# Seven half products for the second matmul of group 4 in a convolution and MLP kernel

## The chip, the core and the metric

The kernel runs on one core of a Trainium2 chip. The metric is the device time of one execution in microseconds (us). Before the change it is 1014.25 us, the median of three runs from 1014.22 to 1014.34. The profile is of a single execution whose span is 1012.3 us.

The names of the engines in the profile: PE is TensorE's matmul and PEld its weight load, DVE is VectorE, ACT is ScalarE, POOL is GpSimd, SP is SyncE, which here only issues transfers.

## What is computed

The input `x` has 8 sequences of 4224 tokens with 192 channels. A causal convolution of seven taps (one set of softmax weights for each of eight heads of 24 channels) gives `x`, and a block with layer norm and two matmuls is added to it:

```python
w = exp(weight - max); w = w / (sum(w) + 1e-09)          # (8 heads, 7 taps)
x = einsum('hk,bskhg->bshg', w, x_unf)                   # the convolution
xn = (x - mu) / np.sqrt(var + 1e-06) * g_ln
ch = np.maximum(xn @ w_ch1, 0.0) @ w_ch2                 # 192 -> 768 -> 192
return x + ch
```

All of it is in float32.

## The kernel before

**Tiling.** Each sequence is spread over 128 partitions, 33 consecutive tokens to a partition. The work goes in 18 groups (`groups`, lines 65 to 73): the first sequence has four small ones (6, 8, 9 and 10 tokens a partition, groups 0 to 3), and every later sequence has one of 16 and one of 17 tokens. Group 4 is the first of the 16-token ones; group 5 follows with 17, group 6 with 16, and so on to group 17.

**Stages of a group.** `load_x` (line 102) brings in the tokens. `first_tap` (line 324, done on ACT at line 336) and `conv` (line 338, DVE, line 346) make the convolution `y`: eight heads by six further taps are 48 DVE instructions. `transpose` (line 351, DVE, line 357) turns `y` in blocks of 32 by 32 into `yt`. `stats` (line 374) computes the scale of each token on DVE. `up` (line 427) is the first matmul: line 457 on TensorE into PSUM tiles `ph`, and line 469 on ACT, the Relu into the hidden tile `ht`. The mean is already taken out of the weights, and the scale is applied to the result afterwards, on ACT at line 624. Then comes the second matmul, which exists in two forms:

- `down` (line 479): the plain one. For each of six blocks of 32 output channels, 24 matmuls at line 493 (six hidden chunks of 128 by four partition blocks of 32) add up into a PSUM tile `po`. `finish` (line 649) has DVE transpose each `po` into the output tile `ot` (line 653).
- `down_fast` (line 537): hidden channels, output channels and tokens are each cut into two halves, and the product of these two-by-two block matrices is made from seven products of half blocks instead of eight, in the manner of Strassen and Winograd. That takes sums of the input halves (DVE, `sums_early` at lines 522 and 523, `sums_late` at 533 and 535), sums of the weight halves (`w2_sums`, line 502, done once), the seven calls of `product` (line 550, matmuls at 555 into PSUM tiles `pd`, and an eviction by ACT at 560 for each of three banks), and sums of the results (DVE, 585 and 598) before the transposes into `ot` (line 600).

**What selects the form.** The table `fast` (lines 76 and 77) gives the number of tokens of each group that go the fast way. Before the change it is 0 for groups 0 to 4 and all tokens for groups 5 to 16; the last group takes 12 of its 17 that way. The table also decides how `up` lays out `ht` and where the Relu writes.

**Order of the work.** The order on each engine is written out by hand: each engine runs its instructions in the order in which the program emits them, and the loop at line 675 is that order. In a group with a fast second matmul the convolution of the next group is cut up, with the sums between its parts; in a group with the plain one it is emitted in one piece. These lines carry it (shortened):

```python
if fast[g]:
    conv(g + 1, 1, 4)
    sums_early(g, (0,))
    conv(g + 1, 4, 5)
    sums_early(g, (1, 2))
    parts = down_fast(g)      # in it: first_tap(g + 2), conv(g + 1, 5, 6), sums_late, line 585
    conv(g + 1, 6, 7)
else:
    conv(g + 1)
transpose(g + 1); store_y(g + 1); stats(g + 1)
# fast: finish_fast(g); plain: down(g), finish(g), first_tap(g + 2)
```

**Buffers.** `yt`, `ht`, `ot`, the sums `s1`, `cs` and `part` have one buffer each, `xg` and `y` two. The eight PSUM banks are shared: `up` takes four at a time, `down` one for each block of channels, `down_fast` six.

Of the kernel before, what the change touches and what calls it, by code (L numbers as in the profile page):

```python
# [16 lines left out]
def kernel(  # L17
# [47 lines left out]
    groups = []  # L65
# [7 lines left out]
    NG = len(groups)  # L73


    fast = {g: groups[g][2] if g >= 5 else 0 for g in range(NG)}
    fast[NG - 1] = J - 5
    NFAST = max(fast.values())
    T = C // 2
# [678 lines left out]
```

## Time and profile before

| | before |
|---|---|
| time, median of 3 runs | 1014.25 us |
| span of the profiled execution | 1012.3 us |
| PE busy | 1000.9 us (99%) |
| DVE busy | 900.4 us (89%) |
| ACT busy | 490.5 us (48%) |
| first matmul (`ph`, L457), share of the chain that ended last | 51.0% |
| half products (`pd`, L555), share of the chain | 35.4% |
| plain second matmul (`po`, L493), share of the chain | 10.3% |

A row of the page's groups names the line, the engine, the operation, the tiles it writes and reads, their shape, and then the busy time of all such instructions, the mean of one in ns, and the idle time of the engine just ahead of them. A float32 matmul leaves two records, so 288 records of L493 are 144 matmuls. The chain that ended last is followed back from the last instruction, at each step to what released it; in order of time it shows in what pieces the span is spent. Where an instruction has a time and an arrow in brackets, its engine stood idle that long before it, and what is named behind the arrow ended the wait.

### The profile page before, as it was taken

To read this page: it belongs to the slowest core of one execution; us is meant where nothing else is said; L and a number is where in the kernel's file an instruction comes from. 1 tells how busy PE (TensorE), PEld (TensorE's weight loads), DVE (VectorE), ACT (ScalarE), POOL (GpSimd) and SP (SyncE) were. 2 spreads that over 40 slices of the span, in tenths; PEclk is the share of its full clock that TensorE was granted. 3 is DMA by queue.
4 is the path that set the end of the run, shared out by engine and by line. 5 is a ranking of instruction groups with operands and counts; after the bars stand their busy time and mean duration, and the time that the engine had idled before them with its cause. 6 is when DMAs were issued, how large, how long until landed. Compare 5 with 4: busy or idle time off the path is not lost.

```text
span 1012.3 us, 34807 instructions
## 1 busy us (share of the span) xinstructions
PE 1000.9 (99%) x15628; PEld 648.8 (64%) x15628; DVE 900.4 (89%) x1766; ACT 490.5 (48%) x1306; POOL 41.1 (4%) x59
## 2 busy tenths in 40 slices
PE   7999999999999999999999999999999999999997
PEld 6887654358545775458754686556854578545786
DVE  7998798955999999999999999989999999999645
ACT  6455344416445454555536455364644546454451
POOL 1001000000000000000000000000000000000000
PEclk9999999999999999999999999999999999999999
DMA  5242550502323433123332331334122343112031
GB/s 196 98 170 63 158 148 38 171 26 44 92 89 59 158 65 150 33 45 150 64 150 50 114 95 33 150 67 159 34 79 104 68 158 64 64 33 37 3 65 69
DMA packets 12068, 91.42 MB, mean 90 GB/s; under 512 B 1679, under 2 KB 2447, under 8 KB 7950
## 3 DMA queue, kind: packets, MB, share of 16 engines
q1 hardware_dynamic: 6718, 64.91, 16.7%
q0 software_dynamic: 4896, 24.28, 14.0%
q8 instruction: 122, 2.00, 0.8%
q14 instruction: 28, 0.23, 0.1%
q10 hardware_dynamic: 304, 0.00, 0.0%
HBM read 38.95 MB, written 50.23 MB: 88 GB/s over the span
## 4 chain that ended last, share of the span: by engine, by line
PE 97%; DVE 2%; DMA 0%; ACT 0%; issue 0%; DVEq 0%; ACTq 0%
PE ph L457 51%; PE pd L555 35%; PE po L493 10%; DVE y L346 1%; DMA taps<-in_weight_dram 0%; DVE y L636 0%; ACT room L266 0%; DVE room L197 0%; DVE yt L357 0%; DVE room L194 0%; ACT room L181 0%; DVE ot L653 0%; ACT room L189 0%; DVE room L186 0%; DVE room L180 0%
## 5 line engine op out<-in xcount | busy, mean ns | idle before, releaser
L457 PE MATMUL ph<-yt,w 32*128 32x256 f32 (+6 forms) x7200 | 517.1, 443 | 1.0 <-DVE yt L357 1.0
L457 PEld LDWEIGHTS ph<-yt,w 32*128 32x128 f32 x7200 | 364.3, 185 | 151.2 <-issue 118.6
L346 DVE SCALAR_TENSOR_TENSOR y<-xg,taps,y 128x384 f32<-128x384 f32 (+5 forms) x852 | 429.0, 580 | 0.0
L469 ACT ACTIVATE ht<-ph 128x256 f32<-128x256 f32 (+6 forms) x600 | 222.7, 457 | 268.9 <-PE ph L457 265.5
L555 PE MATMUL pd<-ht,w 128*32 128x256 f32 (+2 forms) x2808 | 158.0, 382 | 0.0
L555 PE MATMUL pd<-ht,w2sums 128*32 128x256 f32 (+2 forms) x2808 | 155.3, 381 | 0.0
L555 PEld LDWEIGHTS pd<-ht,w 128*32 128x32 f32 x2808 | 89.8, 110 | 66.6 <-issue 7.0
L555 PEld LDWEIGHTS pd<-ht,w2sums 128*32 128x32 f32 x2808 | 91.1, 110 | 61.8
L560 ACT COPY cs<-pd 128x272 f32<-128x272 f32 (+2 forms) x156 | 58.7, 376 | 111.3 <-PE pd L555 111.3
L493 PE MATMUL po<-ht,w 128*32 128x192 f32 (+5 forms) x1728 | 106.0, 406 | 0.0
L522 DVE TENSOR_TENSOR s<-ht 128x1088 f32<-128x1088 f32 (+2 forms) x39 | 48.1, 1233 | 53.5 <-ACT ht L469 53.5
L624 ACT ACTIVATE ot<-ot,r 128x192 f32<-128x192 f32 x247 | 93.1, 471 | 0.0
L493 PEld LDWEIGHTS po<-ht,w 128*32 128x32 f32 x1728 | 55.6, 110 | 49.5 <-issue 22.1
L560 ACT COPY part<-pd 128x272 f32<-128x272 f32 (+2 forms) x117 | 43.9, 375 | 88.0 <-PE pd L555 88.0
L336 ACT ACTIVATE y<-xg,taps 128x384 f32<-128x384 f32 (+5 forms) x142 | 74.1, 591 | 20.7 <-DVE st L371 16.3
L371 DVE BATCH_NORM_STATS2 st<-y 128x6 f32<-128x192 f32 x264 | 69.7, 341 | 0.0
L357 DVE STREAM_TRANSPOSE yt<-y 128x3072 f32<-128x3072 f32 (+5 forms) x18 | 56.0, 3112 | 1.4 <-DVE y L346 0.5
L628 POOL DMA_DIRECT2D out_dram<-ot x34 | 29.5, 883 | 665.6 <-ACT ht L469 348.7
L555 PE MATMUL pd<-s,w2sums 128*32 128x272 f32 (+2 forms) x936 | 53.4, 381 | 0.0
L600 DVE STREAM_TRANSPOSE ot<-cs 128x544 f32<-128x544 f32 (+2 forms) x78 | 50.0, 690 | 2.7 <-ACT cs L560 1.0
L523 DVE TENSOR_TENSOR ht<-ht 128x1088 f32<-128x1088 f32 (+2 forms) x39 | 48.2, 1235 | 2.2
L533 DVE TENSOR_TENSOR ht<-s,ht 128x1088 f32<-128x1088 f32 (+2 forms) x39 | 45.7, 1226 | 0.9 <-PE pd L555 0.9
(75 smaller groups left out, 271.6 us busy)
## 6 DMA issues: line engine op xcount, KB each, us to landing
xg<-in_x_dram SPq DMA_DIRECT2D x7, 2208.0 KB, 12.4
out_dram<-ot POOLq DMA_DIRECT2D x20, 768.0 KB, 6.5
xg<-in_x_dram SPq DMA_DIRECT2D x7, 2112.0 KB, 12.0
out_dram<-y SPq DMA_DIRECT2D x7, 1536.0 KB, 6.0
out_dram<-y SPq DMA_DIRECT2D x6, 1632.0 KB, 6.2
out_dram<-ot POOLq DMA_DIRECT2D x6, 864.0 KB, 6.9
xg<-in_x_dram SPq DMA_DIRECT2D x1, 1536.0 KB, 8.5
xg<-in_x_dram SPq DMA_DIRECT2D x1, 1440.0 KB, 6.9
```

Source lines behind the costliest of these rows:

```text
L336: nc.scalar.mul(dst, src, tap)
L346: nc.vector.scalar_tensor_tensor(out=y[g][:, 0:n, cs], in0=t[:, k : k + n, cs], scalar=taps[:, h, k : k + 1], in1=y[g][:, 0:n, cs], op0=AL ...
L357: nc.vector.transpose(yt[g][:, 0:n].rearrange("p j c t -> p (j c t)"), y[g][:, 0:n].rearrange("p j d -> p (j d)"),)
L371: nc.vector.bn_stats(out=sums[g][:, j, :], in_=y[g][:, j, :])
L457: nc.tensor.matmul(ph[q][:, 0:w], w1[rows, c, fs], t[rows, js, c, :], start=(c == 0), stop=(c == NC - 1),)
L469: nc.scalar.activation(dst, src, AF.Relu)
L493: nc.tensor.matmul(bank[C * q : C * q + C, 0:w], w2[:, f, C * c : C * c + C], t[:, f, q, js.start - fast[g] : js.stop - fast[g], :], start ...
L523: nc.vector.tensor_tensor(a[:, 1, 0, f], a[:, 0, 0, f], a[:, 1, 0, f], op=ALU.subtract)
L555: nc.tensor.matmul(dst[C * q : C * q + C, 0:w], right[:, f, C * c : C * c + C], left[:, f, q], start=(first and f == 0), stop=(f == FC - 1 ...
L560: nc.scalar.copy(to[:, c], dst[:, 0:w].rearrange("p (j t) -> p j t", t=T))
L600: nc.vector.transpose(ot[:, 0:n, C * c : C * c + C], cs[:, c].rearrange("p j h t -> p j (h t)"))
L624: nc.scalar.mul(ots[g][:, j, :], ots[g][:, j, :], rstd[g][:, j : j + 1])
```

## The change

Group 4 gets the fast second matmul too. Its 16 tokens take the seven half products, its Relus write the halved layout, and the convolution of group 5 is cut up around the sums, in the order that groups 6, 8 and so on have. It is meant to spare TensorE an eighth of the multiplications of this group's second matmul. The shape of the buffers does not change.

```diff
-    fast = {g: groups[g][2] if g >= 5 else 0 for g in range(NG)}
+    fast = {g: groups[g][2] if g >= 4 else 0 for g in range(NG)}
     fast[NG - 1] = J - 5
     NFAST = max(fast.values())
```

In the order of the instructions, that replaces on TensorE six runs of 24 matmuls of 512 columns by 252 matmuls of 256 columns. On DVE the 48 instructions of the convolution of group 5 are cut into runs of 24, 8, 8 and 8, with the sums between them, and six transposes at line 653 give way to the sums at 585 and 598 and six transposes at line 600. On ACT 21 evictions are added, and the first tap of group 6 is cut into four pairs between them.

## The prediction

> **What bounds the kernel now.** I read the page first, its busy times and its slices, then the chain of work that ended last, then VectorE (DVE) and ScalarE (ACT) in order of time around group 4. From the page:
>
> ```profile
> PE 1000.9 (99%) x15628; PEld 648.8 (64%) x15628; DVE 900.4 (89%) x1766; ACT 490.5 (48%) x1306; POOL 41.1 (4%) x59
> PE   7999999999999999999999999999999999999997
> DVE  7998798955999999999999999989999999999645
> ```
>
> TensorE is busy in every slice and DVE almost as much, except in slices 4 to 10, above all 9 and 10 (202 to 253 us: the second matmul of group 4 and the start of group 5). So TensorE sets the time, and DVE could take over wherever it gets more work. The chain, in order of time (start, length, what), shows group 4 to the start of group 7:
>
> ```profile
> 157.06 31.11 PE ph L457 x288
> 188.17 31.04 PE po L493 x288
> 219.21 33.21 PE ph L457 x576
> 252.42 29.01 PE pd L555 x504
> 281.43 31.11 PE ph L457 x288
> 312.55 27.33 PE pd L555 x504
> 339.88 33.21 PE ph L457 x576
> ```
>
> Each piece starts where the last one ends. Group 4 has its first matmul (L457) and then the plain second matmul (L493, tile po); group 6, with the same 16 tokens, has the seven half products (L555, tile pd) in its place. From 27.16 to 1005.63 us the chain holds TensorE work alone, so a microsecond less in one of these pieces is a microsecond less in the end, unless TensorE then waits. DVE in order of time, with the waits in brackets:
>
> ```profile
> 166.47 26.69 DVE L346 SCALAR_TENSOR_TENSOR y<-xg,taps,y 128x408 f32<-128x408 f32 x48
> 208.97 0.72 DVE L653 STREAM_TRANSPOSE ot<-po 128x512 f32<-128x512 f32 x1 [2.69 <-PE po L493]
> 214.12 0.72 DVE L653 STREAM_TRANSPOSE ot<-po 128x512 f32<-128x512 f32 x1 [4.43 <-PE po L493]
> 219.28 0.72 DVE L653 STREAM_TRANSPOSE ot<-po 128x512 f32<-128x512 f32 x1 [4.43 <-PE po L493]
> 242.79 1.29 DVE L522 TENSOR_TENSOR s<-ht 128x1088 f32<-128x1088 f32 x1 [10.12 <-ACT ht L469]
> 253.79 1.29 DVE L522 TENSOR_TENSOR s<-ht 128x1088 f32<-128x1088 f32 x1 [1.62 <-ACT ht L469]
> ...
> 304.36 1.23 DVE L522 TENSOR_TENSOR s<-ht 128x1024 f32<-128x1024 f32 x1 [1.44 <-ACT ht L469]
> 314.66 1.23 DVE L522 TENSOR_TENSOR s<-ht 128x1024 f32<-128x1024 f32 x1 [0.92 <-ACT ht L469]
> 333.73 3.58 DVE L357 STREAM_TRANSPOSE yt<-y 128x3264 f32<-128x3264 f32 x1
> ```
>
> In groups 4 and 5 DVE stands idle for 2.69 + 4.43 + 4.43 + 10.12 + 1.62 = 23.29 us. In group 6 it waits only 1.44 and 0.92, both for the Relus that its sums read: that is the settled rhythm, the same at group 16 (1.44 and 0.91).
>
> **What the Trainium skill says.** "Perfetto Trace Analysis", Identifying the Most-Contended Engine, warns that matmul busy share says little of the distance to roofline, while for Vector and Scalar the occupancy serves. Here the first half matters: 99% does not mean that no work can be taken away, and the chain, not the share, shows that the piece counts. "TensorE: Matmul & The Clock Gate", table at its head: ACT and DVE run strictly first in, first out, TensorE alone may pull weight loads ahead. The trace agrees: DVE sits in front of L522 with taps queued behind it, and in the 27.33 us of group 6's products 16.17 us of weight loads lie beside the matmuls. "VectorE: DVE Perf Modes", Side-by-side: one element a cycle in the plain mode plus about 150 cycles of setting up and 8 of fill at 0.96 GHz; for 1024 elements an estimate of 1182 / 0.96 = 1231 ns. The row of L522 with 1024 elements has 1223 ns: agreed, and I use the row.
>
> **The change part by part.**
> TensorE. Out go 144 matmuls of 512 columns (288 records: two for each). In come 7 products x 3 banks x 3 chunks x 4 blocks = 252 matmuls of 256 columns (504 records). In columns that is 64,512 for 73,728, seven eighths, which would turn 31.04 us into 27.16. Group 6 shows 27.33, and groups 8 to 16 (even) as well to 0.01, so each narrower matmul costs a little more than half. I take the measured piece: 31.04 - 27.33 = **3.71 us less**, all on the chain. Group 4's first matmul stays at 31.11, as in group 6.
>
> ACT. Its Relus now write the halved layout. Four of them took 2.07 us together in group 4 (plain) and also in group 16 (halved): nothing. It gains 21 evictions of 0.37 us (7.9 us, L560), and the eight first taps of group 6 move between them. In group 6's products ACT is busy 13.11 of 27.33 us: hidden.
>
> DVE, added. L522, L523, L533 and L535 cost 22.0 + 22.1 + 20.9 + 20.9 = 85.9 us in the six 16-token groups that have them now, 14.3 a group; L585 0.95, the two L598 1.87, the six transposes of L600 3.8; the six of L653 go (4.1). Sum 14.3 + 0.95 + 1.87 + 3.8 - 4.1 = **16.8 us more**. No TensorE time hides this on its own: it must fit into the 23.29 us of idle time, from which the shorter TensorE piece takes 3.71. 23.29 - 16.8 - 3.71 = 2.8 us are left, just about the four waits of the settled rhythm (groups 6 and 7 have 1.44 + 0.92 + 0.24 + 1.55 = 4.15). So DVE should come out level, not late. That is a sum over a stretch, and order decides, so I follow the order.
>
> DVE, in order. The listing of the changed program has, after w2_sums and the statistics of group 4, 24 taps of group 5, sum 1, 8 taps, sums 2 and 3, 8 taps, the late sums, L585, 8 taps, the transpose of group 5. The taps start at 166.47 as now, 9.41 us after group 4's first matmul starts; in group 6 they start at 289.58, 8.15 after. So DVE is 1.26 us behind the rhythm. 24 taps take 13.35 us (half of 26.69): they end at 179.82, offset 22.76. The fourth Relu lets sum 1 start at offset 304.36 - 281.43 = 22.93. The 1.26 us eat the wait of 1.44 and leave 0.17. From sum 1 on group 4 is group 6 moved by 124.37 us: sum 3 waits 0.92 for the last Relu, starts at 190.29, and the transpose of group 5 ends 22.65 us later (337.31 - 314.66 in group 6), at 212.94.
>
> What waits for DVE. The third product needs the sums of L523: in group 6 they end at 317.14 and it starts at 320.27, 3.1 us to spare. The fifth needs L533: 3.2 to spare in group 16. The first matmul of group 5 needs the transpose: 188.17 + 27.33 = 215.50 against 212.94, 2.56 to spare (group 6: 339.88 - 337.31 = 2.57). None of the three waits ends last.
>
> Group 5. DVE finishes group 4's output 10.6 us into group 5's first matmul, as in group 7, not 0.7 as now, so taps of group 6 start 9.9 us later and the wait of 10.12 shrinks to 0.24. That is group 7's value. From there on all is as before, 3.71 us earlier.
>
> Transfers. The store of y of group 5 and the load of x for group 7 behind it go out at about 213 instead of 193.19 and 193.63 us. The load takes 12.4 us; first wanted after group 5's second product, past 255 us. Hidden. w2_sums still ends at 159.2 and is now wanted at 196: hidden. The output tile of group 4 waits for the accumulating stores of group 3, issued by 186.42 and landing in some 5 us, against a first use near 221: nothing.
>
> Sum: 1014.25 - 3.71 = **1010.54 us**, 0.37% faster.
>
> **The rivals.**
> (A) DVE is late at the hand-over. If only the 11.55 us of waits in L653 could be filled and the wait of 10.12 could not, DVE would be 16.84 - 11.55 = 5.29 us late at the transpose of group 5; less the 2.57 to spare, TensorE waits 2.7: 1013.3, no change that can be measured. For it: DVE at 9 tenths in the later slices. Against it: the wait of 10.12 is for Relus of group 5, and the work before it is DVE's own, so it can be filled.
> (B) The sums come after all taps, as the plain order had them. DVE is through with taps, transpose and statistics at 204.4; the early sums take 7.3, to 211.7, while the third product wants them at 196.0: 15.7 us of TensorE wait, 1010.54 + 15.7 = 1026.2, slower. Against it: the listing puts the sums between the taps. For it: only that group 4 has never run in that order.
>
> **How the numbers follow.** Forecast 0.95, A 0.03, B 0.02. Faster than 0.2% is below 1012.2: 0.95; same 0.03; slower 0.02. The low end takes the seven eighths without their surcharge (27.16: 1010.37) less the 0.1 us spread of the runs, 1010.2. The high end allows half a microsecond of TensorE wait at one of the three hand-overs, 1011.1. Both rivals may stay outside.
>
> **What would show it.** In the chain after: a piece of pd with 504 records and about 27.3 us at 188.2, the next ph at 215.5, and the same lengths from there. On DVE: L522 with 1024 elements at about 180.0 with a wait under 0.3, the one at group 5's start with about 0.24 for 10.12, the transpose of group 5 ending near 212.9. DVE busy near 917 us. Wrong if TensorE shows a gap ahead of the third or fifth product of group 4 or of group 5's first matmul, or if group 4's products are longer than group 6's.

## The result and the profile after

The changed kernel takes 1010.83 us (median of 6 runs, 1010.56 to 1010.90) against 1014.24 us beside it (6 runs, 1014.06 to 1015.18). The ratio is 0.9964, with a 95% interval of 0.9952 to 0.9977. The forecast was 1010.54 us, a ratio of 0.9963.

The page, busy times and the slices of DVE:

```profile
PE 997.0 (99%) x15844; PEld 659.5 (65%) x15844; DVE 917.0 (91%) x1781; ACT 497.9 (49%) x1327; POOL 41.2 (4%) x59
...
DVE  7998798999999999999998999989999899999645
```

TensorE is busy for 3.9 us less (1000.9 before), DVE for 16.6 us more (900.4 before). The two slices in which DVE had stood half idle, the ninth and tenth, are full now: the added work lies where the idle time was.

The chain that ended last, in order of time, from group 4 to the start of group 7:

```profile
157.21 31.11 PE ph L457 x288
188.32 27.33 PE pd L555 x504
215.65 33.21 PE ph L457 x576
248.87 29.01 PE pd L555 x504
277.88 31.11 PE ph L457 x288
308.99 27.33 PE pd L555 x504
336.32 33.21 PE ph L457 x576
```

The second piece, 504 records of half products, stands where 31.04 us of L493 stood, and it has the length that group 6 has. Every other piece shown keeps its length to 0.01 us, and each still starts where the one ahead of it ends. From the start of group 4's first matmul to that of group 17's it was 943.23 - 157.06 = 786.17 us and is 939.67 - 157.21 = 782.46 us: **3.71 us less, all of it in that one piece**.

DVE in order of time, from the taps of group 5 on (start, length, what; idle time ahead of it in brackets):

```profile
166.62 13.39 DVE L346 SCALAR_TENSOR_TENSOR y<-xg,taps,y 128x408 f32<-128x408 f32 x24
180.14 1.23 DVE L522 TENSOR_TENSOR s<-ht 128x1024 f32<-128x1024 f32 x1
190.44 1.23 DVE L522 TENSOR_TENSOR s<-ht 128x1024 f32<-128x1024 f32 x1 [0.99 <-ACT ht L469]
...
209.51 3.58 DVE L357 STREAM_TRANSPOSE yt<-y 128x3264 f32<-128x3264 f32 x1
...
239.23 1.29 DVE L522 TENSOR_TENSOR s<-ht 128x1088 f32<-128x1088 f32 x1 [0.24 <-ACT ht L469]
...
250.23 1.29 DVE L522 TENSOR_TENSOR s<-ht 128x1088 f32<-128x1088 f32 x1 [1.55 <-ACT ht L469]
```

Group 4 started 0.15 us later in this execution, so 0.15 comes off each start to compare it with the forecast: the first sum at 179.99 (forecast 180.0, after a wait of 0.17; the view shows 0.13 us between the end of the taps and it and names no wait), the third at 190.29 (190.29), the end of the transpose at 209.51 + 3.58 - 0.15 = 212.94 (212.94). The wait of 10.12 us ahead of group 5's sums has become the 0.24 of group 7. The waits that DVE keeps in groups 4 and 5 are 0.99 + 0.24 + 1.55 = 2.78 us, where the forecast had 2.8 us left over.

### The profile page after: what moved, and what is told of

Same layout as the page of the kernel before. It is cut to its first block, busy times and chain, and to the rows that moved or that the text cites. A ratio compares the mean times of both kernels' runs of the same rounds, so it can differ in the third digit from the quotient of the medians.

```text
span 1008.8 us, 35284 instructions
## 1 busy us (share of the span) xinstructions
PE 997.0 (99%) x15844; PEld 659.5 (65%) x15844; DVE 917.0 (91%) x1781; ACT 497.9 (49%) x1327; POOL 41.2 (4%) x59
## 3 DMA queue, kind: packets, MB, share of 16 engines
q1 hardware_dynamic: 6718, 64.91, 16.8%
## 4 chain that ended last, share of the span: by engine, by line
PE 97%; DVE 2%; DMA 0%; ACT 0%; issue 0%; DVEq 0%; ACTq 0%
PE ph L457 51%; PE pd L555 38%; PE po L493 7%; DVE y L346 1%; DMA taps<-in_weight_dram 0%; DVE y L636 0%; ACT room L266 0%; DVE room L197 0%; DVE yt L357 0%; DVE room L194 0%; ACT room L181 0%; DVE ot L653 0%; ACT room L189 0%; DVE room L186 0%; DVE room L180 0%
## 5 line engine op out<-in xcount | busy, mean ns | idle before, releaser
L457 PE MATMUL ph<-yt,w 32*128 32x256 f32 (+6 forms) x7200 | 517.1, 443 | 1.0 <-DVE yt L357 1.0
L457 PEld LDWEIGHTS ph<-yt,w 32*128 32x128 f32 x7200 | 364.3, 185 | 150.8 <-issue 118.2
L555 PE MATMUL pd<-ht,w 128*32 128x256 f32 (+2 forms) x3024 | 170.2, 381 | 0.0
L555 PE MATMUL pd<-ht,w2sums 128*32 128x256 f32 (+2 forms) x3024 | 167.2, 381 | 0.0
L560 ACT COPY cs<-pd 128x256 f32<-128x256 f32 (+2 forms) x168 | 63.2, 376 | 119.2 <-PE pd L555 119.2
L560 ACT COPY part<-pd 128x256 f32<-128x256 f32 (+2 forms) x126 | 47.2, 375 | 94.5 <-PE pd L555 94.5
L522 DVE TENSOR_TENSOR s<-ht 128x1024 f32<-128x1024 f32 (+2 forms) x42 | 51.8, 1232 | 44.3 <-ACT ht L469 44.1
L493 PE MATMUL po<-ht,w 128*32 128x192 f32 (+4 forms) x1440 | 74.9, 369 | 0.0
L493 PEld LDWEIGHTS po<-ht,w 128*32 128x32 f32 x1440 | 46.9, 110 | 27.2 <-issue 1.0
L555 PE MATMUL pd<-s,w2sums 128*32 128x256 f32 (+2 forms) x1008 | 57.5, 381 | 0.0
L600 DVE STREAM_TRANSPOSE ot<-cs 128x512 f32<-128x512 f32 (+2 forms) x84 | 53.8, 689 | 2.9 <-ACT cs L560 1.0
L523 DVE TENSOR_TENSOR ht<-ht 128x1024 f32<-128x1024 f32 (+2 forms) x42 | 51.9, 1235 | 2.7 <-DVE s L522 0.5
L533 DVE TENSOR_TENSOR ht<-s,ht 128x1024 f32<-128x1024 f32 (+2 forms) x42 | 49.2, 1226 | 0.9 <-PE pd L555 0.9
```

The costliest lines, as they stand in the source:

```text
L457: nc.tensor.matmul(ph[q][:, 0:w], w1[rows, c, fs], t[rows, js, c, :], start=(c == 0), stop=(c == NC - 1),)
L493: nc.tensor.matmul(bank[C * q : C * q + C, 0:w], w2[:, f, C * c : C * c + C], t[:, f, q, js.start - fast[g] : js.stop - fast[g], :], start ...
L523: nc.vector.tensor_tensor(a[:, 1, 0, f], a[:, 0, 0, f], a[:, 1, 0, f], op=ALU.subtract)
L555: nc.tensor.matmul(dst[C * q : C * q + C, 0:w], right[:, f, C * c : C * c + C], left[:, f, q], start=(first and f == 0), stop=(f == FC - 1 ...
L560: nc.scalar.copy(to[:, c], dst[:, 0:w].rearrange("p (j t) -> p j t", t=T))
L600: nc.vector.transpose(ot[:, 0:n, C * c : C * c + C], cs[:, c].rearrange("p j h t -> p j (h t)"))
```

## The experiments

Beside all of them the kernel before ran at medians of 1016.3 to 1017.1 us, not 1014.2, and in their profiles group 4 begins at 159.0 to 160.3 us, not 157.1: the beginning is 2 to 3 us longer there. So ratios are compared, and in the traces the stretch from the start of group 4's first matmul to that of group 17's, which holds nothing of the beginning and the end: 786.17 us before, 782.46 us after. Where code is added, the line numbers behind it move: L458 in such a run is L457 of the kernel.

In the chain a piece is counted from where the one ahead of it ends. In the list of TensorE's instructions in order of time, group 5's first matmul starts about 0.07 us before the last product ends and is longer by as much. This is the changed kernel there, against which the matmuls behind a pause are compared:

```profile
215.58 33.28 PE L457 MATMUL ph<-yt,w 32*128 32x256 f32 x576
```

**The changed kernel once more** (no edit).

> The changed kernel once more, for the kernels beside it. From the start of group 4's first matmul to the start of group 17's the first profile has 782.46 us, 3.71 less than before. Theory: the same to 0.05 us here, and the ratio to the kernel before between 0.996 and 0.997. Rival (the 3.4 us of the first comparison is short of 3.71 because of something in the change): the stretch itself differs.

Ratio 0.9970 (0.9959 to 0.9981), median 1013.13 us against 1016.47. The stretch is 942.48 - 160.02 = 782.46 us, the same to the last digit shown. The interval also holds 0.9963, the ratio for 3.71 us. In the first two profiles, whose spans differ by 3.5 us, what is short of 3.71 lies ahead of the stretch and behind it: 0.15 us in the beginning and 0.07 us in the last half products (20.68 for 20.61).

**Group 6 plain in place of group 4.**

```diff
     fast[NG - 1] = J - 5
+    fast[6] = 0
```

> As the changed kernel, but group 6, also 16 tokens, takes the plain second matmul: groups 4 and 6 have changed places. Theory (the price of the form is 3.71 us of TensorE in any 16-token group that DVE can follow): 1014.5, the time of the kernel before within 0.3. Rival (group 4's place at the start gives it another price): off by more than 1 us.

The chain of this kernel at its group 6 (one more line of code ahead of it, so L493 is L494 here):

```profile
311.01 31.04 PE po L494 x288
```

The stretch is 945.40 - 159.23 = 786.17 us, that of the kernel before exactly: the price of the form is the same 3.71 us in the settled part of the kernel. The ratio, 1.0005 (0.9997 to 1.0013), says no more than "no difference", since the runs of both kernels gather near 1016.3 and near 1017.4 us, and the medians, 1016.29 and 1017.27, came to lie in different places. The kept traces show where such a microsecond can lie: leaving out the runs with group 3, group 4 begins at 159.0 to 159.4 us in the profiles in which the clock granted to TensorE over the first 20 us was 1.00, as in this one, and at 160.0 to 160.3 where it was 0.91. So it seems to belong to the beginning and not to the form of group 6's second matmul.

**The sums after all taps** (rival B): in group 4 the convolution, the transpose and the statistics of group 5 stand ahead of the sums (shortened: in group 4 the later `conv`, `transpose`, `store_y` and `stats` of group 5 are left out, as they have been done).

```diff
+            if g == 4:
+                conv(g + 1); transpose(g + 1); store_y(g + 1); stats(g + 1)
             sums_early(g, (0,))
             ...
             sums_early(g, (1, 2))
             parts = down_fast(g)      # for g == 4 without conv(g + 1, 5, 6)
```

> As the changed kernel, but in group 4 the sums come after the whole convolution, transpose and statistics of group 5 (the order of a plain group). Theory (the gain stands because the order lets DVE's 16.8 us lie in its own idle time): TensorE must wait about 15.7 us ahead of the third product of group 4 (statistics end near 204.5, early sums near 211.8, product wanted at 196.1), about 1026.5 us. Rival (TensorE has room to absorb it, order does not matter): within 1 us of 1010.8.

1029.54 us against 1017.13, ratio 1.0126 (1.0113 to 1.0140). TensorE in order of time, around the third product (the waits in brackets):

```profile
191.13 7.98 PE L555 MATMUL pd<-ht,w 128*32 128x256 f32 x144
210.00 1.08 PE L555 MATMUL pd<-ht,w2sums 128*32 128x256 f32 x8 [10.90 <-DVE ht L523]
212.30 1.08 PE L555 MATMUL pd<-ht,w2sums 128*32 128x256 f32 x8 [1.22 <-DVE ht L523]
214.70 13.49 PE L555 MATMUL pd<-ht,w2sums 128*32 128x256 f32 x200 [1.31 <-DVE ht L523]
```

So the gain hangs on the order, as the theory had it. The waits are 10.90 + 1.22 + 1.31 = 13.43 us and not 15.7, because the product starts on the first sum and doesn't need all three. The products of group 4 take 235.89 - 191.13 = 44.76 us, 17.43 more than 27.33: 4.0 us more than the waits. From 210 to 218 us the clock granted to TensorE was 0.50, from 218 to 222 it was 0.78. The forecast did not have that; see the last section.

**Late sums left out.** Group 4 leaves out L533, L535, L585 and L598; its output lacks them (shortened: the same condition stands ahead of L598).

```diff
+        if g != 4:
             sums_late(g, 0)
             sums_late(g, 1)
             nc.vector.tensor_tensor(c11, c11, part[:, 0], op=ALU.add)
```

> As the changed kernel, but group 4 leaves out the six late sums (L533, L535) and the three result sums (L585, L598), 9.8 us of DVE work; its output lacks them. Theory (none of that work is on the path): 1010.8 within 0.3. Rival (the sums cost the part of 3.71 that the difference of the medians, 3.41, does not show): 1010.5 or less by more than 0.3.

Ratio 0.9967 (0.9956 to 0.9978), stretch 942.71 - 160.25 = 782.46 us: the same. The transpose of group 5 ended 48.26 us after the start of group 4's first matmul for 55.88 in the changed kernel, and nobody used the 7.6 us. Of the added DVE work, these 9.8 us cost nothing at all.

**DVE held up by 9, 13 and 20 instructions**, just ahead of the last eight taps of group 5. They read the weights and write a tile that nobody reads (shortened).

```diff
             parts = down_fast(g)
+            if g == 4:
+                for _ in range(9):      # 13, 20
+                    nc.vector.bn_stats(out=spent, in_=w2flat[:, 0:D])
```

> As the changed kernel, with 9 more bn_stats on DVE (2.39 us at 0.266 each) in group 4, just ahead of the last 8 taps of group 5. Theory (2.56 us to spare at the transpose of group 5): no change, 1010.8 within 0.3. Rival (DVE sets the time already): 2.4 us more, 1013.2.

> As the changed kernel, with 13 more bn_stats on DVE in group 4 ahead of the last 8 taps of group 5. One of them took 0.395 us in the runs with 9 and with 20, so 5.1 us; TensorE then waits 5.1 - 2.56 = 2.6 us for the transpose. Theory (TensorE's clock is halved for a while after a long pause only; the pause of 5.3 us cost 1.6 us more that way, one of 1.0 us nothing): 2.6 us later than the changed kernel and group 5's first matmul 33.2 us long. Rival (each pause costs in proportion, 0.3 us a microsecond): 34.0 us long.

> As the changed kernel, with 20 more bn_stats on DVE (5.31 us) at the same place. Theory: TensorE waits 5.31 - 2.56 = 2.75 us for the transpose of group 5, once, and nothing is made up or lost later: 1013.6. Rival (the later waits of DVE give it back, or every later group pays too): 1010.8, or over 1016.

> The run with 20 more bn_stats and no matmuls in the pause once more, to stand beside the next one on the same chip. Theory: the stretch from group 4's first matmul to group 17's is 789.4 us again, 5.3 us of it pause and 1.6 us a first matmul of group 5 at a lower clock. Rival (the clock fell by chance): the first matmul of group 5 is 33.2 us long.

The ratios are 0.9976 with 9, 0.9993 with 13, and 1.0040 (1.0027 to 1.0052) and 1.0038 (1.0023 to 1.0052) in the two runs with 20. TensorE in order of time with 9, then DVE and TensorE with 13:

```profile
218.44 33.28 PE L458 MATMUL ph<-yt,w 32*128 32x256 f32 x576 [1.00 <-DVE yt L358]
```

```profile
206.92 5.10 DVE L694 BATCH_NORM_STATS2 spent<-w 128x6 f32<-128x192 f32 x13
```

```profile
220.21 33.28 PE L458 MATMUL ph<-yt,w 32*128 32x256 f32 x576 [2.58 <-DVE yt L358]
```

The delay of 5.10 us less the 2.56 that were to spare is 2.54; TensorE waited 2.58. With 9 the delay was 3.51 us, the wait 1.00 us (from 217.44, where the products end, to 218.44) and the stretch 783.53, 1.07 longer: the wait and the overlap of 0.07 us that it undoes. The expectation "no change" for 9 failed by its own size: I had taken 0.266 us for each, from the run of 16 in the kernel, which write 16 places. Those overlap: each lasts 0.34 us. Here all write the same place, each lasts 0.36 us and none starts before the one ahead has ended, so that one takes 0.39. That the shared place is the reason was not tested by itself. With 20 they take 7.86 and 7.87 us, and 7.86 - 2.56 = 5.30 is close to the waits of 5.34 and 5.36 us. Nothing of it was made up later, and no later group paid again. TensorE with 20 and in the repetition:

```profile
222.83 34.82 PE L458 MATMUL ph<-yt,w 32*128 32x256 f32 x576 [5.34 <-DVE yt L358]
```

```profile
222.91 36.32 PE L458 MATMUL ph<-yt,w 32*128 32x256 f32 x576 [5.36 <-DVE yt L358]
```

The matmuls after the pause take 34.82 and 36.32 us for 33.28. The table of stretches (stretch, its length, busy time of PE, PEld, DVE, ACT and POOL, clock granted to TensorE, share and GB/s of the transfers) has the clock beside it, first for the start of the 34.82 us, then for 226 to 230 us of the repetition:

```profile
222.83:226.00 3.17, 3.17 (x31) 2.85 (x35) 3.17 (x14) 0.00 (x0) 0.00 (x0) 0.50 1.02 310
```

```profile
226.00:230.00 4.00, 4.00 (x48) 3.48 (x44) 3.55 (x20) 1.21 (x4) 0.00 (x0) 0.61 1.00 419
```

The clock is at half, in the first run up to 226 us, in the repetition for about 3 us longer. Half speed for 3.17 us of work costs 1.6 us, for 6.2 us 3.1 us: that is the difference between 34.82 and 36.32. In the run with 13 the transfers were as heavy at that point (302 to 418 GB/s), the clock was 1.00 and the piece as long as without a pause, so neither the transfers nor any pause at all costs this, and the cost is not in proportion to the pause: it is a longer pause. The expected 1013.6 us for 20 would be a ratio near 0.999; the measured ones are higher by the longer delay and the clock.

**The pause filled with matmuls** whose result nobody reads, 14 and then 20 (beside the 20 instructions that hold DVE up).

```diff
+                idle = psum.tile([P, 512], F32, tag="ps", name="idle4")
+                for _ in range(14):     # 20
+                    nc.tensor.matmul(
+                        idle[:, 0:P], w2flat[:, 0:P], w2flat[:, P : 2 * P], start=True, stop=True
+                    )
```

> As the run with 20 more bn_stats (pause of 5.3 us, group 5's first matmul 34.82 us instead of 33.21), with 14 matmuls of 128 columns, whose result nobody reads, ahead of group 5's first matmul on TensorE, so that it works through 3 to 4 us of the pause. Theory (the clock drops when TensorE stands still for long): group 5's first matmul starts at the same time as there and is 33.2 us long. Rival (the 1.6 us came from the transfers that ran then, at 310 to 419 GB/s): it stays at 34.8.

> The same delay, with 20 matmuls of 128 columns in the pause instead of 14: 0.242 us each there, 4.8 us, so that less than 1 us of standing still is left. Theory (standing still lowers the clock, and the profile with 14 caught a window with too little work in it): group 5's first matmul 33.2 us long, 1.6 us under the run without them. Rival (these small matmuls do not count as work): 34.8 again.

TensorE with 14, then with 20:

```profile
223.19 34.97 PE L458 MATMUL ph<-yt,w 32*128 32x256 f32 x576 [2.04 <-DVE yt L358]
```

```profile
218.35 4.73 PE L697 MATMUL idle<-w 128*128 128x128 f32 x40
223.77 33.28 PE L458 MATMUL ph<-yt,w 32*128 32x256 f32 x576 [0.69 <-DVE yt L358]
```

Filled with 4.73 us of matmuls, the pause leaves the clock at 1.00, and the piece is 33.28 us long; without them it took 36.32 beside it. Both start 63.8 us after group 4's first matmul, and the transfers are as heavy (315 and 318 GB/s in the first 3 us), so what differs in the traces is the clock. Times: 1018.11 us (ratio 1.0015, 1.0009 to 1.0022) against 1020.91. With 14, 3.39 us of matmuls and 2.04 us of standing still, the profile has 34.97 us and a clock of 0.57 a little later (224.5 to 228.5 us), against the expectation. Its ratio is 1.0021 (1.0012 to 1.0030). Eight of its ten runs, at 1017.86 to 1017.97 and 1018.90 to 1019.14 us, lie about where the runs with 20 lie (1017.71 to 1018.20 and 1018.75 to 1019.24); only the profiled one, 1019.84, and one of 1019.92 lie above. By their times those eight seem to have kept the clock, but only the profiled execution has a trace. A filled pause kept the clock and an empty one of over 5 us lost it; why the pause half filled lost it in this profile is open.

**Group 3 too.** Ten tokens by half products, with the sums of the weights and the statistics of group 3 ahead of its sums.

```diff
-    fast = {g: groups[g][2] if g >= 4 else 0 for g in range(NG)}
+    fast = {g: groups[g][2] if g >= 3 else 0 for g in range(NG)}
...
-        if g == 4:
+        if g == 3:
             w2_sums()
-        if g == 4:
+        if g == 3:
             stats(g)
...
-        elif g < 4:
+        elif g < 3:
             stats(g)
```

> The change taken one group further: group 3 (10 tokens) by half products too, with the sums of the weights and the statistics of group 3 ahead of its sums. TensorE alone: the second matmul of 504 records at 160 columns in place of 19.52 us, an estimate from the pieces of 256 and 192 columns of 17.2 us, so 2.3 us less: rival, 1008.5. Theory (DVE has no idle time there to take the sums of about 12 us): TensorE waits for the third product of group 3 (about 5 us), the fifth (2) and for the transpose of group 4 (3 to 4), 8 to 9 us more than the changed kernel, about 1019.

1021.64 us against 1016.29, ratio 1.0051 (1.0037 to 1.0064). TensorE:

```profile
147.99 0.48 PE L555 MATMUL pd<-ht,w2sums 128*32 128x160 f32 x8 [3.15 <-DVE ht L523]
149.59 8.67 PE L555 MATMUL pd<-ht,w2sums 128*32 128x160 f32 x200 [1.12 <-DVE ht L523]
...
166.54 32.88 PE L457 MATMUL ph<-yt,w 32*128 32x512 f32 x288 [3.39 <-DVE yt L357]
```

4.27 us of waits at the third product and 3.39 at the transpose, and two pieces longer than they need be: the clock was 0.73 from 149.6 to 155.9 us and 0.56 from 166.5 to 170, and group 4's first matmul took 32.88 us for 31.18 in the same view of the changed kernel. From the start of group 3's first matmul to that of group 4's it is 46.66 us (119.88 to 166.54), against 157.21 - 118.10 = 39.11 in the changed kernel, and the 1.70 come on top: 9.3 us more. The same step that gave 3.71 us in group 4 costs 9.3 in group 3, where DVE has little idle time to give: in the changed kernel it waits 2.43 us just ahead of these 39 us and 2.05 us near their end, and not in between.

**Group 3 with its late sums on GpSimd**, and the statistics of group 3 and the sums of the weights moved ahead of the transposes of group 2's output (shortened).

```diff
+            eng = nc.gpsimd if g == 3 else nc.vector
             if e == 0:
-                nc.vector.tensor_tensor(dst[:, f], less[:, f], dst[:, f], op=ALU.subtract)
+                eng.tensor_tensor(dst[:, f], less[:, f], dst[:, f], op=ALU.subtract)
...
         elif g < 3:
             stats(g)
+            if g == 2:
+                stats(3)
+                w2_sums()
```

> Group 3 by half products too, in another order: the statistics of group 3 and the sums of the weights move into DVE's idle time ahead of the transposes of group 2's output, and the six late sums of group 3 run on GpSimd. TensorE alone gives about 2.1 us less than the changed kernel. Theory (with the DVE work moved out, the transpose of group 4 ends at about 36.3 us into the 36.9 that TensorE needs): 2.1 us less, about 0.9945 of the kernel before. Rival (GpSimd is too slow for the fifth and seventh product, or slows DVE): no gain over the changed kernel, or a loss.

1019.81 us against 1016.47, ratio 1.0031 (1.0019 to 1.0044): the theory fell, and of the rival the second half holds, that GpSimd slows DVE. DVE in order of time while GpSimd works (141.78 to 153.7 us) and just after:

```profile
142.01 2.18 DVE L522 TENSOR_TENSOR s<-ht 128x640 f32<-128x640 f32 x1
...
146.20 9.51 DVE L346 SCALAR_TENSOR_TENSOR y<-xg,taps,y 128x384 f32<-128x384 f32 x8
...
156.20 4.31 DVE L346 SCALAR_TENSOR_TENSOR y<-xg,taps,y 128x384 f32<-128x384 f32 x8
```

Eight taps took 9.51 us beside GpSimd and 4.31 after it; a sum of 0.82 us took 2.18. The six sums took GpSimd 11.1 us. The Trainium skill, "SBUF — State Buffer", SBUF: two separate sides, has DVE instructions with two inputs and GpSimd ones that read SBUF take turns on one pair of ports, the loser standing still. The numbers agree, though nothing in this run separates the ports from another cause. DVE got rid of 4.6 us of sums and lost some 8. TensorE then waited 5.83 us for the transpose and ran group 4's first matmul in 34.02 us. No version here beats the changed kernel.

## Why the prediction was right

**TensorE's piece.** 31.04 - 27.33 = 3.71 us, read off group 6, is what the stretch shows in two executions of the changed kernel, and group 6 made plain takes the same amount back. Seven eighths of the columns alone would have said 3.88.

**DVE's added work.** 16.8 us were reckoned from the rows and 16.6 measured on the page (917.0 - 900.4). That all of it was hidden rests on the whole change costing no wait; the run without the late sums shows it for 9.8 us by itself.

**The order on DVE.** Moving group 6's rhythm by the difference of the starts, and checking that the 1.26 us of delay at the beginning fits into a wait of 1.44, gave the transpose to 0.01 us. The three delays measured the room behind it: 1.00, 2.58 and 5.34 us of wait for 3.51, 5.10 and 7.86 us of delay are 2.5 us of room each time, where 2.56 was read.

**Rival A** (DVE late) had the wait of 10.12 us as one that cannot be filled. It was filled, 0.24 us are left of it, and TensorE waits nowhere in the changed piece. **Rival B** (sums behind the taps) is what the other order does; its wait was put 2.3 us too high, since the product starts on the first sum, and the halved clock was left out.

**What was off.** The store of group 5's y was put at 213 us, the end of the transpose. It waits for the last tap, not for the transpose, and went out at 209.50. Nothing hung on it. The median is 0.29 us above the forecast. The profiled execution took 1010.56 us, and the runs of this kernel lie between that and 1010.90; where the others spent more was not traced. So the median came within 0.3 us, but what the traces confirm to 0.01 us is the changed piece.

## What to carry to other kernels

Where the chain is one engine without gaps, the price of another form can be read from a neighbour that already has it. What then has to be shown is that the other engines can follow: sum their added work against the idle time in the same stretch, and then follow the order instruction by instruction up to each hand-over, because here the same instructions in another order cost 12 us where they had saved 3.4. The next step of the same kind can lose: the idle time that paid for group 4 is used up, and group 3 has little of it.

## What the runs showed of the hardware

A pause of TensorE can cost more than its length. After pauses of 1.00 and 2.58 us group 5's first matmul took 33.28 us, the same as without a pause; after pauses of 5.34 and 5.36 us it took 34.82 and 36.32. In the experiment with group 3 a pause of 3.39 us was enough: a clock of 0.56 for 3.5 us, 1.70 us lost.

The time at half clock came in steps. Where the table of stretches is cut finely, the clock is 1.00 or 0.50, and something between only in a stretch in which it changes; the mean there gives an estimate of the moment. With 20 instructions of delay it was at half from 222.6 to 226.0 us, which is 3.4 us, and in the repetition from 222.3 to 229.1, which is 6.8. With the sums last it was 17.1 us (202.7 to 219.8), about five times 3.4; there it fell 3.6 us after TensorE had stopped and stayed down through the later waits. The other four falls, two with group 3, one with GpSimd and one in the pause half filled, lasted 3.4, 3.4, 6.8 and 3.4 us. So the same pause can cost 1.5 us or 3.0.

The Trainium skill, "TensorE: Matmul & The Clock Gate", Part 1: The HAM clock gate, gives about 3.4 us of idleness for the drop to half speed and about as long to come back. The pauses fit it: 2.58 us, below it, without a drop, 3.39, just at it, and 5.34 with one. The way back agrees in the first run with 20, 3.2 us after TensorE started again, and not in the repetition, 6.2 us. Two drops are not explained by these runs: the one in group 3's third product, behind pauses of 3.15 and 1.12 us with 0.48 us of matmuls between them, and the one behind the pause half filled with small matmuls, which was empty for 2.04 us only.
